# A new hand-written order and more choices of engine in a block-sparse attention and channel-mix kernel

## The chip, the cores and the metric

The kernel runs on one core of one Trainium2 chip. The metric is the device time of one execution in microseconds (us). Its engines are TensorE (PE in the rows; PEld is its weight load), VectorE (DVE), ScalarE (ACT), GpSimd (POOL) and SyncE (SP), which issues every DMA here.

## The reference

Two layers follow each other. The first is block-sparse attention: 4 batches, 8 heads, 768 positions in 24 blocks of 32, head size 64. A query block sees its neighbours, the first and last block, and three blocks drawn at random; the first and the last query block see everything.

```python
scores = scale * np.matmul(q, k.transpose(0, 1, 3, 2))
mask = np.abs(blk_i - blk_j) <= window
mask = mask | (blk_i == 0) | (blk_j == 0) | (blk_i == n_blocks - 1) | (blk_j == n_blocks - 1)
...
attn = attn / (np.sum(attn, axis=-1, keepdims=True) + 1e-09)
return np.matmul(attn, v).astype(np.float32)
```

The second mixes channels of its output x (4 x 768 x 512) with the position before:

```python
xk = mu_k * x + (1.0 - mu_k) * x_prev
xr = mu_r * x + (1.0 - mu_r) * x_prev
k = np.maximum(xk @ w_k, 0.0)
v = k * k @ w_v
r = 1.0 / (1.0 + np.exp(-(xr @ w_r)))
return (r * v).astype(np.float32)
```

w_k is 512 x 1024, w_v 1024 x 512, w_r 512 x 512; all three come as 8-byte floats.

## The kernel before, in words

**Attention** goes in 26 units. Units 0 to 21 each take one query block of all four batches (near units); units 22 to 25 take the first and last block of one batch (wide units). A near unit is a chain: load queries, keys and values; two score steps on PE (tile s, L400, 64 recorded matmuls in all: an fp32 matmul of the program is recorded as two); a row maximum on DVE (tile nm, L410); four exponentials on ACT (tile p); a transpose on DVE (tile r, L453); a DMA that moves it (tile pt); two value steps on PE (tile o, L473, 128 recorded matmuls; L434 in units 0 to 2); the division on DVE, and a turn of x into the mixer's tile xt ("put x").

**The mixer** takes 12 tiles of 256 positions. For each, xk and xr are mixed (ACT "now", DVE "mix", L663) and split into a high and a low part ("hi" on ACT, "lo" on POOL, L672). PE then computes r (gate, tile r_0p or r_1p, 12 matmuls of 512 columns a half tile, L696), h (hidden, four tiles h_0p to h_3p of 24 matmuls of 256 columns, L713) and v (values, 24 matmuls of 512 columns a half tile, in 8 steps of 3, L742). Between h and v stand relu and "hi" on ACT, "square" (L728) and "lo" (L730) on POOL. PE's result tiles of the mixer take turns in two buffers of one tag, "m".

**Weights**: 20 pieces w0 to w19 are converted from 8-byte floats on DVE, ACT and POOL (size, tail, sign, join, hi, lo) early in the program.

**The order.** Each step is recorded by plan.add with its engine, an estimated time and its buffers. The list ORDER then names the steps one by one, and they are issued in just that order, engine by engine; CHOICE names the engine of a step that is recorded by choose with several ways. Nothing is planned at run time: a step waits on its engine until its inputs and buffers are there, and all steps behind it on that engine wait too.

**PE's instruction stream.** A recorded matmul is two instructions, a weight load and a matmul. With the waits on semaphores that stand between them the built program before has 14,654 instructions on PE, one straight stream without loops.

Of the kernel before, what the change touches and what calls it, by code (L numbers as in the profile page):

```python
# [15 lines left out]
ALU = mybir.AluOpType  # L16
# [4 lines left out]
B, H, S, D = 4, 8, 768, 64  # L21
# [74 lines left out]
def block_sparse_attention_channel_mix(  # L96
# [3 lines left out]
    nc = tc.nc  # L100
# [13 lines left out]
    def choose(name, ways, **more):  # L114

        way = CHOICE.get(name, 0)
        engine, ns, port, fn = ways[way]
        plan.add(name, engine, ns, fn, port=port, ways=[w[:3] for w in ways], **more)
# [45 lines left out]
    def warm(times, ns):  # L164
        w = buf([P, 512], F32, "m", M_BUFS, f"warm{times}", ps)

        def run():
            one = nc.const_aps.tensor(1.0, (P, 512), BF16)
            for i in range(times):
                nc.tensor.matmul(w.ap, one[:, 0:P], one, start=(i == 0), stop=(i == times - 1))  # L170

        plan.add("warm", PE, ns * times, run, writes=[(w,)], code=2 * times)
# [4 lines left out]
    def weight(i, name, src):  # L177
# [37 lines left out]
        choose(f"w{i} tail", [(DVE, 338, 338, tail), (POOL, 650, 0, tail_pool), (ACT, 600, 0, tail_act)], reads=[(raw,)], writes=[(f, 0)])  # L215
# [13 lines left out]
        choose(f"w{i} sign", [(DVE, 338, 338, sign), (ACT, 600, 0, sign_act), (POOL, 650, 0, sign_pool)], reads=[(raw,)], writes=[(f, 1)])  # L229
# [151 lines left out]
    def near_unit(at, q, first, o):  # L381
# [6 lines left out]
        for gi in range(2):  # L388
# [30 lines left out]
            for i in range(4):  # L419
                row, a = divmod(i, 2)  # L420
                plan.add(f"u{name} exp {i}", ACT, 420, lambda p=p, s=s, nm=nm, row=row, a=a, i=i: nc.scalar.activation(
                    p.ap[:, i * 256 : (i + 1) * 256].rearrange("p (c x j) -> p c x j", c=2, j=QB),
                    s.ap[:, row, a * 256 : (a + 1) * 256].rearrange("p (c j x) -> p c x j", c=2, j=QB), AF.Exp, bias=nm.ap[:, i : i + 1], scale=SCALE),
                    reads=[(s,), (nm,)], writes=[(p, i)], table="exp")
# [120 lines left out]
    def finish(at, members, o, parts):  # L545
# [3 lines left out]
        for i in range(len(o)):  # L549
# [7 lines left out]
            plan.add(f"u{at} {i} recip", DVE, 275, recip, reads=[(o[i], *parts)], writes=[(R, i)])  # L557
# [12 lines left out]
            plan.add(f"u{at} {i} divide", DVE, 430, divide, reads=[(o[i], *parts), (R, i)], writes=[(x, i)])  # L570
        n = members[0][1]
        if moved:
# [4 lines left out]
            def move():  # L577
                for b in range(B):
# [4 lines left out]
            plan.add(f"u{at} put x", ACT, 467, lambda: nc.scalar.copy(to.ap[:, :, n % 2, :, 1:], xm.ap.rearrange("p b c x -> p c b x")),  # L583
                     reads=[(xm,)], writes=[(to, n)])
# [11 lines left out]
        if not n:  # L596
# [12 lines left out]
        plan.add(f"u{at} put x", ACT, 467, lambda: nc.scalar.copy(  # L609
            to.ap[:, :, n % 2, :, 1:], tp.ap.rearrange("p c (b x) -> p c b x", b=B)), reads=[(tp,)], writes=[(to, n)])  # L610
# [27 lines left out]
    def split_x(t, which, i0, many, name):  # L638
# [14 lines left out]
        for h in range(CC // MIX):  # L653
            f = buf([P, MIX, tw], F32, "mix", 1, f"{name}f{h}")
            for i in range(MIX):
# [6 lines left out]
                def mix(d=d, c=c, i=i, f=f):  # L662
# [7 lines left out]
            plan.add(f"{name} hi {h}", ACT, 66 + 0.895 * MIX * tw, lambda f=f, cs=cs: nc.scalar.copy(dst.ap[:, 0, cs], f.ap),  # L670
                     reads=[(f, *range(MIX))], writes=[(dst, (0, h))])
            plan.add(f"{name} lo {h}", POOL, 160 + 2.17 * MIX * tw, lambda f=f, cs=cs: nc.gpsimd.tensor_tensor(  # L672
                out=dst.ap[:, 1, cs], in0=f.ap, in1=dst.ap[:, 0, cs], op=ALU.subtract),
                reads=[(f, *range(MIX)), (dst, (0, h))], writes=[(dst, (1, h))])
# [15 lines left out]
    def gate(name, xr, z, last):  # L690
# [12 lines left out]
        plan.add(f"{name} out", ACT, 475, lambda: nc.scalar.copy(z.ap, pr.ap[:, 0:512]), reads=[(pr,)], writes=[(z,)])  # L703

    def hidden(name, xk, k2, f2, last):
# [17 lines left out]
        def lo():  # L723
# [4 lines left out]
        plan.add(f"{name} square", POOL, 1000, lambda: nc.gpsimd.tensor_tensor(out=kk.ap, in0=kk.ap, in1=kk.ap, op=ALU.mult),  # L728
                 reads=[(kk,)], writes=[(kk,)])
        plan.add(f"{name} lo", POOL, 1245, lambda: nc.gpsimd.tensor_tensor(out=lo(), in0=kk.ap, in1=hi(), op=ALU.subtract),  # L730
                 reads=[(kk,), (k2, (0, f2))], writes=[(k2, (1, f2))])
# [74 lines left out]
MIX = 2  # L806
# [9 lines left out]
}  # L816
ORDER = [
# [128 lines left out]
```

## Time and profile before

| | |
|---|---|
| Runs (us) | 538.75, 540.99, 534.01; median 538.75 |
| Profiled execution | 541.3 us, span 539.4 us |
| Mean granted TensorE clock | 0.978 |
| PE / DVE / ACT / POOL busy (us) | 486.6 / 291.5 / 327.0 / 215.4 |
| Matmuls recorded | 7260 |
| DMA | 115.68 MB, 214 GB/s |

The span runs from the first to the last instruction; the execution's own time is 1.9 us longer. Busy time of PE is modelled from pipelined matmuls, so the time of a stretch of matmuls is best read from the start of its first row to the start of the next row.

### The profile page before, as it was taken

The page shows a single profiled execution, that of the slowest core. Times are in us where ns is not written, and L with a number is a line of the kernel's source. Part 1 is how long each engine was busy: PE and PEld are TensorE (multiplying, and loading weights), DVE is VectorE, ACT ScalarE, POOL GpSimd, SP SyncE. Part 2 cuts the span into 40 slices and gives each one's busy share as a digit, 9 for nine tenths or more (in the row PEclk, how much of TensorE's full clock was granted, in tenths as well). Part 3 has the DMA queues.
Part 4 walks back from the last instruction along what each step waited for, and adds up shares of the span by engine and source line. Part 5 has one row for each costly group of instructions (what it writes and reads, how often), then busy time and mean ns, then how long its engine had stood idle before and what let it go on. Part 6 is the DMA issues. An engine that isn't in the chain of part 4 may idle for free.

```text
span 539.4 us, 17745 instructions
## 1 busy us (share of the span) xinstructions
PE 486.6 (90%) x7260; PEld 398.7 (74%) x7260; DVE 291.5 (54%) x560; ACT 327.0 (61%) x749; POOL 215.4 (40%) x208
## 2 busy tenths in 40 slices
PE   0585999899999999998999996998999999999997
PEld 0253578668887778786887885877878878888896
DVE  3795879655655653666355565466454363222221
ACT  4685878756664665676484575492644866455541
POOL 4464556212521712442620641351441632726361
PEclk9996999998999999999999999899999999999999
DMA  8999699897878888787798888489966655101001
GB/s 286 403 377 396 203 343 296 272 259 213 235 220 221 259 222 236 237 245 232 219 254 235 243 217 281 116 258 279 307 187 182 222 118 133 46 2 39 21 21 39
DMA packets 58627, 115.68 MB, mean 214 GB/s; under 512 B 7729, under 2 KB 20785, under 8 KB 55602
## 3 DMA queue, kind: packets, MB, share of 16 engines
q1 hardware_dynamic: 58546, 114.55, 69.8%
q8 instruction: 57, 0.93, 0.7%
q14 instruction: 24, 0.20, 0.1%
HBM read 77.82 MB, written 6.29 MB: 156 GB/s over the span
## 4 chain that ended last, share of the span: by engine, by line
PE 68%; DMA 9%; SPq 7%; issue 5%; DVE 5%; ACT 4%; POOL 0%; DVEq 0%; ACTq 0%; POOLq 0%
PE v L742 19%; PE s L400 7%; PE h_1p L713 6%; PE h_0p L713 6%; PE o L473 5%; PE r_1p L696 5%; PE h_3p L713 5%; PE r_0p L696 5%; PE h_2p L713 4%; DMA pt<-r 3%; SPq L461 3%; PE o L536 2%; PE sw L494 2%; DMA KA<-kt 2%; DVE r L453 2%
## 5 line engine op out<-in xcount | busy, mean ns | idle before, releaser
L742 PE MATMUL v<-w,k 128*128 128x512 f32 (+1 forms) x600 | 140.3, 386 | 0.0
L742 PEld LDWEIGHTS v<-w,k 128*128 128x128 f32 x600 | 107.6, 188 | 25.0 <-issue 1.8
L400 PE MATMUL s<-KA,q 64*32 64x256 f32 x1408 | 54.2, 424 | 27.3 <-DMA KA<-kt 18.2
L450 ACT ACTIVATE p<-s,nm 128x256 f32<-128x256 f32 x152 | 65.0, 478 | 1.6 <-DVE R L554 0.8
L400 PEld LDWEIGHTS s<-KA,q 64*32 64x32 f32 x1408 | 28.1, 116 | 45.0 <-issue 18.5
L410 DVE TENSOR_REDUCE nm<-s 128x4 f32<-128x1024 f32 x44 | 53.1, 1214 | 14.8 <-PE s L400 14.6
L453 DVE STREAM_TRANSPOSE r<-p 128x1024 f32<-128x1024 f32 x38 | 46.1, 1229 | 12.4 <-DMA pt<-r 6.7
L473 PE MATMUL o<-VA,pt 128*32 128x65 f32 x2432 | 41.5, 221 | 10.8 <-issue 8.2
L672 POOL TENSOR_TENSOR xr<-xr_0f,xr 128x256 fp32r<-128x256 f32 x24 | 17.8, 742 | 83.2 <-ACT xr L670 76.4
L473 PEld LDWEIGHTS o<-VA,pt 128*32 128x32 f32 x2432 | 36.7, 109 | 19.1 <-issue 14.4
L663 DVE SCALAR_TENSOR_TENSOR xr_1f<-xt,mk,xr_1d 128x128 f32<-128x128 f32 x48 | 21.9, 457 | 41.9 <-ACT xr_1d L660 24.7
L672 POOL TENSOR_TENSOR xr<-xr_1f,xr 128x256 fp32r<-128x256 f32 x24 | 17.8, 743 | 55.3 <-ACT xr L670 55.3
L713 PE MATMUL h_0p<-xk,w 128*128 128x256 f32 x288 | 38.9, 290 | 0.5 <-DVE w L244 0.3
L713 PEld LDWEIGHTS h_0p<-xk,w 128*128 128x128 f32 x288 | 36.7, 195 | 3.2 <-issue 1.2
L565 DVE TENSOR_TENSOR x<-o,R 128x128 f32<-128x128 f32 x96 | 25.0, 323 | 25.2 <-ACT xt L583 11.9
L713 PE MATMUL h_1p<-xk,w 128*128 128x256 f32 x288 | 37.9, 287 | 0.0
L713 PE MATMUL h_3p<-xk,w 128*128 128x256 f32 x288 | 37.6, 284 | 0.0
L713 PE MATMUL h_2p<-xk,w 128*128 128x256 f32 x288 | 37.5, 284 | 0.0
L713 PEld LDWEIGHTS h_1p<-xk,w 128*128 128x128 f32 x288 | 36.1, 194 | 1.6 <-DVE xr_1f L663 0.8
L663 DVE SCALAR_TENSOR_TENSOR xr_0f<-xt,mk,xr_0d 128x128 f32<-128x128 f32 x48 | 17.8, 371 | 35.5 <-ACT xr_0d L660 16.1
L713 PEld LDWEIGHTS h_3p<-xk,w 128*128 128x128 f32 x288 | 35.7, 190 | 1.4 <-issue 0.8
L696 PE MATMUL r_0p<-w,xr 128*128 128x512 f32 x144 | 36.2, 398 | 0.5 <-POOL xr L672 0.5
(174 smaller groups left out, 842.4 us busy)
## 6 DMA issues: line engine op xcount, KB each, us to landing
VA<-vt SPq DMA_DIRECT2D x92, 260.0 KB, 4.3
KA<-kt SPq DMA_DIRECT2D x89, 256.0 KB, 4.1
pt<-r SPq DMA_DIRECT2D x76, 256.0 KB, 4.9
VA<-vw SPq DMA_DIRECT2D x24, 260.0 KB, 5.1
KA<-kq SPq DMA_DIRECT2D x16, 384.0 KB, 5.9
ptw<-rw SPq DMA_DIRECT2D x32, 192.0 KB, 3.9
out<-z SPq DMA_DIRECT2D x23, 256.0 KB, 4.2
q<-qt SPq DMA_DIRECT2D x22, 256.0 KB, 4.6
```

The source lines that it names most:

```text
L400: nc.tensor.matmul(s.ap[ROWS[j], row, a * 256 : (a + 1) * 256].rearrange("p (n x) -> p n x", x=BLK), q.ap[half, (hp * QB + j) * BLK : (hp ...
L410: nc.vector.tensor_reduce(out=nm.ap.rearrange("p (r a) -> p r a", r=2), in_=s.ap.rearrange("p r (a x) -> p r a x", a=2), axis=AX.X, op=ALU ...
L450: plan.add(f"u{name} exp {i}", ACT, 365, lambda row=row, a=a, i=i: nc.scalar.activation(squares()[:, :, :, i, :], s.ap[:, row, a * 256 : ( ...
L453: plan.add(f"u{name} turn", DVE, N_TURN, lambda: nc.vector.transpose(out=r.ap[:, :, gi].rearrange("p j c i x -> p j (c i x)"), in_=squares ...
L461: nc.sync.dma_start(pt.ap[:, b].rearrange("p g c i x -> p (g c i x)"), r.ap[ROWS[b]].rearrange("p j g c i x -> p j (g c i x)"))
L473: nc.tensor.matmul(o[gi].ap[ROWS[j], i * DV : (i + 1) * DV], pt.ap[:, j, gi, g, 2 * row + a, :], VA.ap[:, c0 + g, j, h * DV : (h + 1) * DV ...
L565: nc.vector.tensor_tensor(out=to[:, :, 2 * e : 2 * e + 2], in0=o[i].ap.rearrange("p (c e v) -> p c e v", e=2, v=DV)[:, :, e, 0:D].rearrang ...
L663: nc.vector.scalar_tensor_tensor(out=parts(f.ap[:, i, :]), in0=cols(c, 1), scalar=mk.ap[:, 2 + which, c : c + 1], in1=parts(d.ap), op0=ALU ...
L672: plan.add(f"{name} lo {h}", POOL, 160 + 2.17 * MIX * tw, lambda f=f, cs=cs: nc.gpsimd.tensor_tensor(out=dst.ap[:, 1, cs], in0=f.ap, in1=d ...
L696: nc.tensor.matmul(pr.ap[:, 0:512], xr.ap[:, a, c, :], weight_of["r", c].ap[:, w, :], start=(c == 0 and m == 0), stop=(c == CC - 1 and m = ...
L713: nc.tensor.matmul(ph.ap[:, ff * TT : (ff + 1) * TT], weight_of["k", c, f2 // 2].ap[:, w, f % 4 * P : (f % 4 + 1) * P], xk.ap[:, a, c, :], ...
L742: nc.tensor.matmul(pv.ap[:, 0:width], k2.ap[:, a, f, i * P : (i + 1) * P], weight_of["v", f].ap[:, w, cs], start=(f == 0 and m == 0), stop ...
```

## The change

The 2,106 steps and what they compute stay the same. ORDER is a new list, CHOICE another table, and steps of 13 kinds stand on another engine. Against before, in the built program: 32 "lo" and 21 "square" of h go from POOL to DVE; 24 "lo" of xr and 15 of xk from POOL to DVE; 22 "hi" of xr and 12 of xk from ACT to POOL; 14 copies of r out of PSUM ("r out") and 8 "put x" from ACT to DVE; some 46 conversion steps of the weights and 5 "turned" copies between ACT, DVE and POOL. The warm-up matmuls are 10 instead of 20 and stand in another place. Estimates of time (ns) that the list was made with are changed too; they have no effect on the program.

```diff
-        def run():
+        def run(times):
...
-        plan.add("warm", PE, ns * times, run, writes=[(w,)], code=2 * times)
+        choose("warm", [(PE, ns * many, 0, lambda many=many: run(many)) for many in (times, times // 2, 1)], writes=[(w,)], code=2 * (times, times // 2, 1)[CHOICE.get("warm", 0)])
...
+            choose(f"{name} hi {h}", [
+                (ACT, 66 + 0.895 * MIX * tw, 0, lambda f=f, cs=cs: nc.scalar.copy(dst.ap[:, 0, cs], f.ap)),
+                (POOL, 50 + 1.05 * MIX * tw, 0, lambda f=f, cs=cs: nc.gpsimd.tensor_copy(dst.ap[:, 0, cs], f.ap)),
+            ], reads=[(f, *range(MIX))], writes=[(dst, (0, h))])
+            choose(f"{name} lo {h}", [
+                (POOL, 160 + 2.17 * MIX * tw, 0, lambda rest=rest: rest(nc.gpsimd)),
+                (DVE, 63 + 1.06 * MIX * tw, 63 + 1.06 * MIX * tw, lambda rest=rest: rest(nc.vector)),
+            ], reads=[(f, *range(MIX)), (dst, (0, h))], writes=[(dst, (1, h))])
...
+        choose(f"{name} out", [
+            (ACT, 475, 0, lambda: nc.scalar.copy(z.ap, pr.ap[:, 0:512])),
+            (DVE, 600, 0, lambda: nc.vector.tensor_copy(out=z.ap, in_=pr.ap[:, 0:512])),
+        ], reads=[(pr,)], writes=[(z,)])
...
+        choose(f"{name} square", [
+            (POOL, 1000, 0, lambda: nc.gpsimd.tensor_tensor(out=kk.ap, in0=kk.ap, in1=kk.ap, op=ALU.mult)),
+            (DVE, 603, 603, lambda: nc.vector.tensor_tensor(out=kk.ap, in0=kk.ap, in1=kk.ap, op=ALU.mult)),
+        ], reads=[(kk,)], writes=[(kk,)])
+        choose(f"{name} lo", [
+            (POOL, 1245, 0, lambda: nc.gpsimd.tensor_tensor(out=lo(), in0=kk.ap, in1=hi(), op=ALU.subtract)),
+            (DVE, 603, 603, lambda: nc.vector.tensor_tensor(out=lo(), in0=kk.ap, in1=hi(), op=ALU.subtract)),
+        ], reads=[(kk,), (k2, (0, f2))], writes=[(k2, (1, f2))])
...
 ORDER = [
-    3, 4, 1, 961, 7, 16, 933, 934, 935, 936, 937, 938, 11, 14, 939, 982, 975, 964, 13, 978, 962, 984, 963, 977, 985, 10, 976, 979, 8, 5, 12, 20, 9, 965, 966, 980, 15, 919, 55,
+    3, 4, 11, 0, 13, 1, 7, 919, 16, 9, 975, 921, 1045, 12, 978, 976, 1046, 961, 14, 10, 1048, 5, 1047, 977, 1049, 979, 980, 981, 962, 1050, 964, 963, 965, 1051, 920, 982, 922,
```

First place: PE around the scores of unit 7. o5_0 and o5_1 are the values of unit 5, s7_0 and s7_1 the scores of unit 7, v1 the values of mixer tile 1; a row of x16 or x32 is recorded as twice as many matmuls. Before:

```order
L742 MATMUL v1_0_0_1488<-w18_1561,k21_1219 128x512 x3
L473 MATMUL o5_0_1613<-VA_68,pt5_1496 32x65 x32
L473 MATMUL o5_1_1651<-VA_68,pt5_1496 32x65 x32
L400 MATMUL s7_0_1688<-KA_67,q7_1231 32x256 x16
L400 MATMUL s7_1_1705<-KA_67,q7_1231 32x256 x16
L742 MATMUL v1_1_0_1726<-w12_661,k21_1219 128x512 x3
```

Of the change:

```order
L759 MATMUL v1_1_0_1517<-w17_749,k21_1292 128x512 x3
L472 MATMUL o5_0_1606<-VA_68,pt5_1558 32x65 x32
L472 MATMUL o5_1_1639<-VA_68,pt5_1558 32x65 x32
L759 MATMUL v1_0_0_1568<-w15_873,k21_1292 128x512 x3
L759 MATMUL v1_1_0_1517<-w18_1555,k21_1292 128x512 x3
L759 MATMUL v1_1_0_1517<-w19_127,k21_1292 128x512 x3
L399 MATMUL s7_0_1712<-KA_67,q7_1454 32x256 x16
L399 MATMUL s7_1_1731<-KA_67,q7_1454 32x256 x16
```

Nine matmuls of 512 columns now stand between the values and the scores, which stood back to back.

Second place: PE around the values of unit 19 (o19) and the scores of unit 21 (s21). Before:

```order
L696 MATMUL r7_0p_5262<-w3_97,xr7_0_5200 128x512 x3
L473 MATMUL o19_0_5278<-VA_68,pt19_5229 32x65 x32
L473 MATMUL o19_1_5330<-VA_68,pt19_5229 32x65 x32
L400 MATMUL s21_0_5365<-KA_67,q21_4904 32x256 x16
L400 MATMUL s21_1_5382<-KA_67,q21_4904 32x256 x16
```

Of the change:

```order
L706 MATMUL r7_0p_5253<-w3_361,xr7_0_5026 128x512 x3
L726 MATMUL h7_0p_5238<-xk7_4898,w4_1036 128x256 x3
L726 MATMUL h7_0p_5238<-xk7_4898,w5_1166 128x256 x3
L726 MATMUL h7_0p_5238<-xk7_4898,w6_1148 128x256 x3
L726 MATMUL h7_0p_5238<-xk7_4898,w7_171 128x256 x3
L472 MATMUL o19_0_5296<-VA_68,pt19_5276 32x65 x32
L472 MATMUL o19_1_5334<-VA_68,pt19_5276 32x65 x32
L399 MATMUL s21_0_5401<-KA_67,q21_5329 32x256 x16
L399 MATMUL s21_1_5424<-KA_67,q21_5329 32x256 x16
```

Here values and scores still follow each other; twelve matmuls of h now stand between r7_0 and the values, and 14 more recorded matmuls stand ahead of o19_1 in the program.

Third place: DVE around the row maxima of unit 10 (nm10). Before:

```order
L453 STREAM_TRANSPOSE r9_2371<-p9_1_2232 128x4x256
L410 TENSOR_REDUCE nm10_0_2395<-s10_0_2354 128x4
L663 SCALAR_TENSOR_TENSOR xr3_0f0_2491<-xt3_1724,mk_70,xr3_0d1_2350 128x128
L748 SCALAR_TENSOR_TENSOR z2_0_1844<-v2_0_0_2284,z2_0_1844 128x512
L453 STREAM_TRANSPOSE r9_2371<-p9_0_2133 128x4x256
```

Of the change:

```order
L675 TENSOR_TENSOR xr3_0_2228<-xr3_0f0_2361,xr3_0_2228 128x256
L452 STREAM_TRANSPOSE r9_2445<-p9_1_2333 128x4x256
L765 SCALAR_TENSOR_TENSOR z2_1_2230<-v2_1_0_2298,z2_1_2230 128x512
L409 TENSOR_REDUCE nm10_0_2520<-s10_0_2486 128x4
L666 SCALAR_TENSOR_TENSOR xr3_1f0_2522<-xt3_1563,mk_70,xr3_1d0_2467 128x128
L409 TENSOR_REDUCE nm10_1_2539<-s10_1_2503 128x4
L715 COPY z3_0_2568<-r3_0p_2525 128x512
```

The row L675 is a "lo" that was POOL's, the row L715 an "r out" that was ACT's; both now stand in DVE's queue among the attention's steps.

## Rows read from the trace of the kernel before

**Rows 1.** The page: span, and busy us of each engine.

```profile
span 539.4 us, 17745 instructions
...
PE 486.6 (90%) x7260; PEld 398.7 (74%) x7260; DVE 291.5 (54%) x560; ACT 327.0 (61%) x749; POOL 215.4 (40%) x208
```

**Rows 2.** Windows: stretch and length, busy us by engine, granted clock, DMA share, GB/s.

```profile
16.75:60.00 43.25, 30.54 (x699) 19.45 (x699) 33.46 (x62) 31.21 (x76) 21.51 (x23) 0.84 0.95 358
60.00:100.00 40.00, 38.25 (x616) 29.37 (x617) 34.04 (x59) 30.73 (x73) 24.09 (x22) 1.00 0.93 295
100.00:340.00 240.00, 223.30 (x3793) 183.72 (x3791) 135.71 (x267) 149.25 (x354) 79.16 (x75) 0.98 0.83 238
340.00:536.20 196.20, 194.54 (x2156) 166.10 (x2156) 81.39 (x158) 107.99 (x237) 83.37 (x78) 0.99 0.45 131
```

**Rows 3.** Waits of PE on "issue": us in total, times, longest.

```profile
PE o L473 <- issue: 8.2, 5, 4.4
PE s L400 <- issue: 7.7, 6, 1.7
PE o L434 <- issue: 4.2, 1, 4.2
```

**Rows 4.** The page's DMA queues: packets, MB, share of 16 engines.

```profile
q8 instruction: 57, 0.93, 0.7%
```

**Rows 5.** Timeline of PE, 90 to 140: start, us, operation; idle before in brackets.

```profile
90.67 3.02 PE L696 MATMUL r_1p<-w,xr 128*128 128x512 f32 x12
93.53 0.85 PE L742 MATMUL v<-w,k 128*128 128x512 f32 x3
...
101.01 2.04 PE L473 MATMUL o<-VA,pt 128*32 128x65 f32 x128
102.97 1.49 PE L400 MATMUL s<-KA,q 64*32 64x256 f32 x39
105.93 1.07 PE L400 MATMUL s<-KA,q 64*32 64x256 f32 x25 [1.46 <-issue]
106.93 6.52 PE L742 MATMUL v<-w,k 128*128 128x512 f32 x27
...
130.06 3.00 PE L713 MATMUL h_1p<-xk,w 128*128 128x256 f32 x24
132.99 1.96 PE L400 MATMUL s<-KA,q 64*32 64x256 f32 x64
134.88 1.80 PE L473 MATMUL o<-VA,pt 128*32 128x65 f32 x110
137.09 0.53 PE L473 MATMUL o<-VA,pt 128*32 128x65 f32 x18 [0.41 <-issue]
137.55 3.11 PE L713 MATMUL h_3p<-xk,w 128*128 128x256 f32 x24
```

**Rows 6.** The chain in order of time, 116 to 127: start, us, what.

```profile
122.40 4.44 PE h_0p L713 x24
```

**Rows 7.** Timeline of PE, 336 to 344.

```profile
336.06 0.32 PE L473 MATMUL o<-VA,pt 128*32 128x65 f32 x1 [4.42 <-issue]
336.31 3.67 PE L400 MATMUL s<-KA,q 64*32 64x256 f32 x64
339.90 3.97 PE L713 MATMUL h_1p<-xk,w 128*128 128x256 f32 x24
```

**Rows 8.** Timeline of PE, 65 to 71: the warm-up matmuls.

```profile
65.36 4.55 PE L170 MATMUL warm<-const-bfloat16-1.0 128*128 128x512 bf16 x20
...
70.71 0.30 PE L473 MATMUL o<-VA,pt 128*32 128x65 f32 x2 [0.37 <-DMA pt<-r]
```

**Rows 9.** Groups of DVE instructions: busy us, mean ns, idle before by releaser.

```profile
L410 DVE TENSOR_REDUCE nm<-s 128x4 f32<-128x1024 f32 x44 | 53.1, 1214 | 14.8 <-PE s L400 14.6 <-ACT pt L373 0.2
L453 DVE STREAM_TRANSPOSE r<-p 128x1024 f32<-128x1024 f32 x38 | 46.1, 1229 | 12.4 <-DMA pt<-r 6.7 <-ACT p L450 3.9 <-DMA q<-qt 1.6
L748 DVE SCALAR_TENSOR_TENSOR z<-v,z 128x512 f32<-128x512 f32 x23 | 15.8, 687 | 19.1 <-PE v L742 14.0 <-ACT z L775 4.1 <-ACT p L450 0.7
```

More of the change, by code (lines that the diff above doesn't have):

```diff
@@ L114, in choose @@
     def choose(name, ways, **more):
-        way = CHOICE.get(name, 0)
-        engine, ns, port, fn = ways[way]
+        engine, ns, port, fn = ways[CHOICE.get(name, 0)]
         plan.add(name, engine, ns, fn, port=port, ways=[w[:3] for w in ways], **more)
@@ L213, in tail_act @@
                 nc.scalar.activation(halves(U16, 0), shorts(1), AF.Copy, scale=2.0**-13, bias=2.0**-14 - 0.5)
-        choose(f"w{i} tail", [(DVE, 338, 338, tail), (POOL, 650, 0, tail_pool), (ACT, 600, 0, tail_act)], reads=[(raw,)], writes=[(f, 0)])
+        choose(f"w{i} tail", [(DVE, 338, 338, tail), (POOL, 900, 0, tail_pool), (ACT, 640, 0, tail_act)], reads=[(raw,)], writes=[(f, 0)])
         def sign():
@@ L227, in sign_pool @@
                 nc.gpsimd.tensor_scalar(out=halves(F16, 1), in0=high().bitcast(F32), scalar1=2.0**-60, scalar2=None, op0=ALU.mult)
-        choose(f"w{i} sign", [(DVE, 338, 338, sign), (ACT, 600, 0, sign_act), (POOL, 650, 0, sign_pool)], reads=[(raw,)], writes=[(f, 1)])
+        choose(f"w{i} sign", [(DVE, 338, 338, sign), (ACT, 630, 0, sign_act), (POOL, 1650, 0, sign_pool)], reads=[(raw,)], writes=[(f, 1)])
         def join():
@@ L420, in near_unit @@
                 row, a = divmod(i, 2)
-                plan.add(f"u{name} exp {i}", ACT, 420, lambda p=p, s=s, nm=nm, row=row, a=a, i=i: nc.scalar.activation(
+                plan.add(f"u{name} exp {i}", ACT, 365, lambda p=p, s=s, nm=nm, row=row, a=a, i=i: nc.scalar.activation(
                     p.ap[:, i * 256 : (i + 1) * 256].rearrange("p (c x j) -> p c x j", c=2, j=QB),
@@ L555, in recip @@
                 nc.vector.reciprocal(r, r)
-            plan.add(f"u{at} {i} recip", DVE, 275, recip, reads=[(o[i], *parts)], writes=[(R, i)])
+            plan.add(f"u{at} {i} recip", DVE, 330, recip, reads=[(o[i], *parts)], writes=[(R, i)])
             def divide(i=i, each=each):
@@ L568, in divide @@
                         in1=R.ap[:, each, :].rearrange("p (c e) (z o) -> p c e z o", e=2, z=1)[:, :, e].to_broadcast([P, 2, 2, BLK]), op=ALU.mult)
-            plan.add(f"u{at} {i} divide", DVE, 430, divide, reads=[(o[i], *parts), (R, i)], writes=[(x, i)])
+            plan.add(f"u{at} {i} divide", DVE, 460, divide, reads=[(o[i], *parts), (R, i)], writes=[(x, i)])
         n = members[0][1]
@@ L582, in finish @@
             to, then = tile_of(n // 2), tile_of((n + 1) // 2)
-            plan.add(f"u{at} put x", ACT, 467, lambda: nc.scalar.copy(to.ap[:, :, n % 2, :, 1:], xm.ap.rearrange("p b c x -> p c b x")),
-                     reads=[(xm,)], writes=[(to, n)])
+            choose(f"u{at} put x", [
+                (ACT, 467, 0, lambda: nc.scalar.copy(to.ap[:, :, n % 2, :, 1:], xm.ap.rearrange("p b c x -> p c b x"))),
+                (DVE, 600, 600, lambda: nc.vector.tensor_copy(out=to.ap[:, :, n % 2, :, 1:], in_=xm.ap.rearrange("p b c x -> p c b x"))),
+            ], reads=[(xm,)], writes=[(to, n)])
             plan.add(f"u{at} put z", ACT, 80, lambda: nc.scalar.copy(
@@ L608, in finish @@
         to = tile_of(n // 2)
-        plan.add(f"u{at} put x", ACT, 467, lambda: nc.scalar.copy(
-            to.ap[:, :, n % 2, :, 1:], tp.ap.rearrange("p c (b x) -> p c b x", b=B)), reads=[(tp,)], writes=[(to, n)])
+        choose(f"u{at} put x", [
+            (ACT, 467, 0, lambda: nc.scalar.copy(to.ap[:, :, n % 2, :, 1:], tp.ap.rearrange("p c (b x) -> p c b x", b=B))),
+            (DVE, 600, 0, lambda: nc.vector.tensor_copy(out=to.ap[:, :, n % 2, :, 1:], in_=tp.ap.rearrange("p c (b x) -> p c b x", b=B))),
+        ], reads=[(tp,)], writes=[(to, n)])
         then = tile_of((n + 1) // 2)
@@ L669, in split_x, with rest @@
             cs = slice(h * MIX, (h + 1) * MIX)
[L670 to L674, printed above, removed]
+            def rest(by, f=f, cs=cs):
+                by.tensor_tensor(out=dst.ap[:, 1, cs], in0=f.ap, in1=dst.ap[:, 0, cs], op=ALU.subtract)
+            choose(f"{name} hi {h}", [
[6 more added lines that the diff above has]
+            ], reads=[(f, *range(MIX)), (dst, (0, h))], writes=[(dst, (1, h))])
         return dst
@@ L702, in gate @@
                      reads=[(xr, *SPLIT), *[(weight_of["r", c], 0, 1) for c in cs]], writes=[(pr,)], code=12)
-        plan.add(f"{name} out", ACT, 475, lambda: nc.scalar.copy(z.ap, pr.ap[:, 0:512]), reads=[(pr,)], writes=[(z,)])
+        choose(f"{name} out", [
+            (ACT, 475, 0, lambda: nc.scalar.copy(z.ap, pr.ap[:, 0:512])),
+            (DVE, 600, 0, lambda: nc.vector.tensor_copy(out=z.ap, in_=pr.ap[:, 0:512])),
+        ], reads=[(pr,)], writes=[(z,)])
     def hidden(name, xk, k2, f2, last):
@@ L727, in hidden @@
         plan.add(f"{name} hi", ACT, 522, lambda: nc.scalar.activation(hi(), kk.ap, AF.Square), reads=[(kk,)], writes=[(k2, (0, f2))])
[L728 to L731, printed above, removed]
+        choose(f"{name} square", [
[6 more added lines that the diff above has]
+        ], reads=[(kk,), (k2, (0, f2))], writes=[(k2, (1, f2))])
     def values(t, i, k2, z, last):
```

159 rows, old and new, of tables (CHOICE, ORDER) are left out of this document.

## The prediction

> **What bounds the kernel now.** I read the windows first, because the limits differ by stage. TensorE (PE) is busy 486.6 of 539.4 us [rows 1], so 52.8 us of idle time are what an order can win. Of them 16.7 lie before the first scores, 12.7 from there to 60 us (43.25 less 30.54, at a DMA share of 0.95 and a clock of 0.84), 1.8 up to 100, 16.7 between 100 and 340, 1.7 after that, and 3.2 behind the last matmul [rows 2]. The early part belongs to the transfers, the late part is full. So I looked at the 16.7 us between 100 and 340, where DVE is busy 136 of 240 us and the DMA share is 0.83: nothing else is full there.
>
> The waits give the cause: PE waited 15.9 us on "issue" (8.2 and 7.7, eleven times) in scores and values of moved units, and 4.2 us once in L434 [rows 3]. "Issue" is time in which an engine waits for nothing that the profile shows. In the timeline such a pause cuts a run of equal matmuls in two, 39 scores and 25 scores of one unit [rows 5]: their inputs were there, or the first would not have run. What was missing is the instructions. The instruction queue carried 57 packets in 0.93 MB [rows 4], 16 KB each; the program has 14,654 instructions on PE, 257 to a packet. I counted the instructions of the program up to each pause: all twelve stand at number 449 to 451 beyond a multiple of 512, so at every second packet. I call these places borders; there are 28.
>
> Not every border pauses. Ahead of those that do, the 256 instructions (128 matmuls) before the border are all scores and values, which run fast: values 1.96 us for 128 (101.01 to 102.97), scores 1.89 for 64 (132.99 to 134.88) [rows 5]. With 89 values and 39 scores the 128 take 2.5 us. Where 12 matmuls of r (some 2.8 us, 0.23 each) lie among them, as at 94 us, PE goes on at once [rows 5]. So I take it that a packet is asked for about when those 256 begin, and comes late if they last less than it needs. Adding the time of the 256 to the pause behind them gives what each of the eleven needed: 2.8 to 4.9 us for ten, 6.6 for the one at 336.06 [rows 7].
>
> The Trainium skill says otherwise ("Runtime: NRT & Kernel Launch", section Instruction fetch mechanics): fetch streams ahead in blocks of 256 instructions and is hidden, and PE holds 2048 of them. The block size agrees with [rows 4]; the hidden fetch does not, by the eleven pauses of [rows 3]. By that rule the spacing of this order would be worth nothing; it is a rival below.
>
> **The change part by part.**
>
> Borders. With the same 512 and the same offset I counted where the borders fall in the new order, and added up the 128 matmuls before each at the rates above (v and r 0.23 us, h 0.12). At the fifteen borders from unit 7 to unit 19, which had 2.0 to 2.9 us, now 4.3 to 7.6 us lie ahead: nine v matmuls between values and scores at unit 7, twelve of h before the values of unit 19. If the packet needs what it needed, ten of eleven would have 0.4 us or less to wait, and the long one 1 to 2. Spread over fifteen borders that is about 3 us left.
>
> What is taken away is more than the 15.9 us of idle time, since a row's end is modelled: from 102.97 to 106.93 a unit's scores take 3.96 us against 1.89, a pause of 2.07 where the bracket says 1.46; from 134.88 to 137.55 the values take 2.67 against 1.96, 0.71 where it says 0.41 [rows 5]. Half of 0.61 and 0.30 is 0.45, for eleven pauses 5 us. **So 20.9 us go, and 3 stay.**
>
> The clock. After the long pause PE is slow: 64 scores take 3.67 us against 1.96, 24 matmuls of h 3.97 against 3.00 [rows 5, 7], and after the pause at 120 us 24 of h take 4.44 [rows 6]. Together 1.7 + 1.0 + 1.4, **4 us, go with the pauses.** In the stretch the granted clock is 0.98 [rows 2].
>
> Head borders. The pause in L434 (4.2 us) stands where 105 values and 19 scores now come before the border: 2.7 us, as before. I leave it. One border on, at unit 4's scores, 12 matmuls of r lay ahead; these have gone behind the scores, and 2.6 us are left, against 4.1 in the middle of the needs. **Plus 1.6 us**, bounds 0 and 4.2.
>
> Warm-up. Ten matmuls of 4.55/20 us less stand in the stream; the ten that stay are early, where PE waits anyway. What they covered is the wait for unit 3's move, still 0.37 us at 70.71 [rows 8]. That move is 0.5 MB earlier in SP's queue, 1.5 us at 358 GB/s [rows 2]. So **minus 1.5 us** of the 2.3; bounds 0 and 2.3.
>
> The transfers of the head. Up to unit 0's drawn keys 4.82 MB are queued instead of 4.56, 0.7 us later; up to unit 2's drawn values 17.1 instead of 18.2, 3 us earlier; unit 0's and 1's values stay. **Nothing**, bounds 3 us either way. That PE's early steps are covered by transfers hides the new order of weight conversions too; without that cover their bound would be the 12.7 us of idle time.
>
> Steps on another engine. A 128 x 512 step on DVE takes 0.69 us [rows 9]. The 53 steps of h and 15 of xk are 47 us, 24 of xr at half the size 8, 14 "r out" and 8 "put x" 15: DVE goes from 291 to about 361 us, 70% of the span. Of that some 35 fall into 100 to 340, 171 of 220 us there. POOL and ACT get lighter. On PE's path this costs nothing so long as DVE has slack; that cover is 49 us in that stretch.
>
> New waits. A stretch that is 20 us shorter asks the same transfers in less time: 0.83 x 240/220 is a share of 0.91. Between 60 and 100 the share is 0.93 and PE idles 1.8 of 40 us [rows 2], which over 220 us would be 10; at the share of now it is the 0.8 us that are not "issue". I take **plus 4 us**, bounds 0 and 10, nearer the low end because DVE, which is at 85% between 60 and 100, is less full here.
>
> Sum: 539.4 - 20.9 - 4 + 3 + 1.6 - 1.5 + 4 = 521.6 us of span, 523.5 with the 1.9 us around it. The profiled execution, 541.3 us, is 2.55 above the median of 538.75, so I forecast **521 us**. The bounds around it: residual pauses 0 to 9 (half of the old ones), new waits 0 to 10, head 4 either way, hence 512 to 531.
>
> **The rivals.**
>
> *More is won.* If no new waits and no residual pauses come and the head border falls away too, the 3, the 4, the 1.6 and 4.2 us more go: about 508 to 512. For it: PE idles only 1.8 us from 60 to 100, where more borders lie and a slow product stands before each [rows 2]. Against: a packet needed over 6 us twice, here and in the head. 15%.
>
> *Half is won.* The packets share the DMA engines with data; at a share of 0.91 they come later, and the transfers behind PE's steps bind in place of the fetches (new waits of 10 us, pauses of 7). Then 521 + 6 + 4, about 531. For it speaks the idle time at 0.93; against, PE's 38 of 40 us there. 17%.
>
> *It does not do what it says.* The pauses would be something else than fetches and come at other places, as many as before: 538.75 - 1.5, about 537. Against it are twelve of twelve pauses at one remainder. 3%. The section of the Trainium skill that is named above leads to this case.
>
> *Slower.* DVE becomes what PE waits for. PE's mixer results take turns in two buffers; fourteen of them, the "r out", now wait in DVE's queue behind a row maximum (1.21 us) and a transpose (1.23 us) [rows 9], where ACT emptied them. Once DVE runs a whole product (2.8 us) late, each of the fourteen holds PE for up to 2.4 us, 34 in all: 521 + 34 = 555. It decides from the point at which DVE is over some 95% busy in a stretch; the fullest now is 85% [rows 2], and the middle would be 78%. 6%.
>
> **How the numbers follow.** The forecast has 59%. For the range, 511 to 533 holds nearly all of the forecast's own 512 to 531, half of the first rival and most of the second; about 0.17 is left out. Faster by over 2% means below 528, which is about what a measurement here can tell: 0.53 of the forecast, 0.15, and 0.06 of the half win give 0.74. Within 2%: 0.06, 0.11 and 0.03, so 0.20. Slower 0.06.
>
> **What would show it.** PE's waits on "issue" from 100 on fall from 15.9 us to under 5; PE is busy over 95% between 100 and 320, at a granted clock of 0.99 or more; the last unit's scores start 20 us sooner. DVE's busy time rises to some 360 us, and no wait of PE for DVE is over 2 us in total. If the pauses stay where the count puts the borders, though 4 us and more lie ahead, the reading of how long a packet needs is wrong; if they come elsewhere, the reading of borders is. If PE waits for DMA by over 10 us after 60 us, the half win is right.

## The result, and the profile after

| | before | changed |
|---|---|---|
| Runs (us), median | 539.87 (4 runs) | 522.42 (519.11 to 523.59, 4 runs) |
| Ratio | | 0.9702, 95% interval 0.9605 to 0.9799 |
| Profiled execution, span | 541.3, 539.4 | 523.59, 521.8 |
| Mean granted clock | 0.978 | 0.984 |

The change makes the kernel faster by 3.0%; 521 us was forecast. The profiled execution of the kernel before is one of its slower ones (its runs took 534.0 to 546.1 us). The page of the changed kernel, span and busy us of each engine, answers to [rows 1]:

```profile
span 521.8 us, 17723 instructions
...
PE 481.7 (92%) x7250; PEld 396.1 (76%) x7250; DVE 349.0 (67%) x675; ACT 304.4 (58%) x695; POOL 129.8 (25%) x147
```

Its windows answer to [rows 2]. The middle stretch is drawn 20 us shorter; some 110 recorded matmuls more lie behind its end than before, which cost the last stretch 1.2 us of busy time:

```profile
16.00:60.00 44.00, 31.26 (x716) 19.63 (x722) 35.75 (x69) 31.63 (x76) 20.02 (x22) 0.91 0.96 354
60.00:100.00 40.00, 35.68 (x589) 28.89 (x589) 33.31 (x60) 30.56 (x71) 16.11 (x15) 0.93 0.96 306
100.00:320.00 220.00, 218.52 (x3681) 181.73 (x3685) 160.99 (x315) 136.32 (x325) 45.23 (x49) 1.00 0.86 248
320.00:518.00 198.00, 195.77 (x2283) 165.53 (x2273) 110.95 (x217) 99.17 (x215) 42.59 (x49) 0.99 0.49 142
```

From 100 to 320 us PE idles 1.5 us, where it idled 16.7 between 100 and 340. The gain is there. From 60 to 100 it idles 4.3 us instead of 1.8, and the clock is 0.93 instead of 1.00: some of it is given back. Ahead of 60 us it is the other way round, 0.91 where it was 0.84. PE's waits on "issue", against [rows 3] (the 2.1 us are 0.64 at 38, 1.09 at 92 and 0.38 at 137 us):

```profile
PE o L433 <- issue: 3.8, 1, 3.8
PE s L399 <- issue: 2.1, 3, 1.1
```

The timeline of PE at unit 7, where [rows 5] had 1.46 us of idle inside the scores, and at unit 19, where [rows 7] had 4.42 us inside the values:

```profile
103.65 2.03 PE L472 MATMUL o<-VA,pt 128*32 128x65 f32 x128
105.61 2.38 PE L759 MATMUL v<-w,k 128*128 128x512 f32 x9
107.92 1.96 PE L399 MATMUL s<-KA,q 64*32 64x256 f32 x64
109.81 1.67 PE L759 MATMUL v<-w,k 128*128 128x512 f32 x6
...
317.74 1.55 PE L726 MATMUL h_0p<-xk,w 128*128 128x256 f32 x12
319.23 2.03 PE L472 MATMUL o<-VA,pt 128*32 128x65 f32 x128
321.76 1.96 PE L399 MATMUL s<-KA,q 64*32 64x256 f32 x64 [0.51 <-DMA KA<-kt]
323.65 3.12 PE L726 MATMUL h_3p<-xk,w 128*128 128x256 f32 x24
```

The 64 scores take 1.96 us at both places (3.67 after the long pause before), and 24 of h 3.12 instead of 3.97: the clock stays up. What is lost stands at 60, 93 and 98 us:

```profile
59.93 3.80 PE L399 MATMUL s<-KA,q 64*32 64x256 f32 x64 [1.05 <-ACT xt L611]
63.66 4.04 PE L706 MATMUL r_0p<-w,xr 128*128 128x512 f32 x12
...
91.46 0.64 PE L399 MATMUL s<-KA,q 64*32 64x256 f32 x9
93.19 1.93 PE L399 MATMUL s<-KA,q 64*32 64x256 f32 x55 [1.09 <-issue]
...
99.96 0.51 PE L759 MATMUL v<-w,k 128*128 128x512 f32 x1 [1.47 <-ACT xt L615]
```

Three waits of 0.5 to 1.1 us come close together at 56 to 60 us, and from 59.1 to 65.9 us the granted clock is 0.50, the lower of its two levels: scores and r run at about half speed, some 2.8 us more than at full clock. Unit 6's scores have a pause that they did not have, and at 98 us the values wait 1.5 us for "put z" on ACT (L615), the step that hands the last position of each block of x to the next tile.

### The profile page after: what moved, and what is told of

Its sections match the earlier page's. It is cut to its first block, busy times and chain, and to the rows that moved or that the text cites. A ratio compares the mean times of both kernels' runs of the same rounds, so it can differ in the third digit from the quotient of the medians.

```text
span 521.8 us, 17723 instructions
## 1 busy us (share of the span) xinstructions
PE 481.7 (92%) x7250; PEld 396.1 (76%) x7250; DVE 349.0 (67%) x675; ACT 304.4 (58%) x695; POOL 129.8 (25%) x147
## 4 chain that ended last, share of the span: by engine, by line
PE 66%; SPq 11%; DMA 9%; ACT 6%; DVE 4%; issue 4%; POOL 0%; DVEq 0%; ACTq 0%; POOLq 0%
PE v L759 18%; PE s L399 6%; PE h_3p L726 6%; PE r_1p L706 5%; PE h_2p L726 5%; PE h_1p L726 5%; PE r_0p L706 5%; PE h_0p L726 5%; SPq L460 5%; PE o L472 4%; DMA KA<-kt 4%; PE o L535 2%; PE sw L493 2%; SPq L578 2%; DMA xm<-rx 1%
## 5 line engine op out<-in xcount | busy, mean ns | idle before, releaser
L399 PE MATMUL s<-KA,q 64*32 64x256 f32 x1408 | 49.8, 408 | 21.4 <-DMA KA<-kt 17.9
L449 ACT ACTIVATE p<-s,nm 128x256 f32<-128x256 f32 x152 | 63.5, 478 | 0.6
L472 PE MATMUL o<-VA,pt 128*32 128x65 f32 x2432 | 39.9, 221 | 1.5 <-DMA pt<-r 1.4
L666 DVE SCALAR_TENSOR_TENSOR xr_1f<-xt,mk,xr_1d 128x128 f32<-128x128 f32 x48 | 17.8, 371 | 30.4 <-ACT xr_1d L663 28.1
L726 PE MATMUL h_0p<-xk,w 128*128 128x256 f32 x288 | 37.8, 286 | 0.0
L726 PEld LDWEIGHTS h_2p<-xk,w 128*128 128x128 f32 x288 | 35.4, 190 | 1.6 <-ACT h_0k L739 0.6
L706 PE MATMUL r_1p<-w,xr 128*128 128x512 f32 x144 | 36.5, 399 | 0.0
L726 PE MATMUL h_1p<-xk,w 128*128 128x256 f32 x288 | 36.4, 282 | 0.0
L706 PEld LDWEIGHTS r_0p<-w,xr 128*128 128x128 f32 x144 | 27.2, 194 | 7.2 <-issue 1.2
```

Of the source, the lines that this page charges most:

```text
L399: nc.tensor.matmul(s.ap[ROWS[j], row, a * 256 : (a + 1) * 256].rearrange("p (n x) -> p n x", x=BLK), q.ap[half, (hp * QB + j) * BLK : (hp ...
L449: plan.add(f"u{name} exp {i}", ACT, 365, lambda row=row, a=a, i=i: nc.scalar.activation(squares()[:, :, :, i, :], s.ap[:, row, a * 256 : ( ...
L472: nc.tensor.matmul(o[gi].ap[ROWS[j], i * DV : (i + 1) * DV], pt.ap[:, j, gi, g, 2 * row + a, :], VA.ap[:, c0 + g, j, h * DV : (h + 1) * DV ...
L666: nc.vector.scalar_tensor_tensor(out=parts(f.ap[:, i, :]), in0=cols(c, 1), scalar=mk.ap[:, 2 + which, c : c + 1], in1=parts(d.ap), op0=ALU ...
L706: nc.tensor.matmul(pr.ap[:, 0:512], xr.ap[:, a, c, :], weight_of["r", c].ap[:, w, :], start=(c == 0 and m == 0), stop=(c == CC - 1 and m = ...
L726: nc.tensor.matmul(ph.ap[:, ff * TT : (ff + 1) * TT], weight_of["k", c, f2 // 2].ap[:, w, f % 4 * P : (f % 4 + 1) * P], xk.ap[:, a, c, :], ...
```

## The experiments

Theory A says that the gain is that of the instruction fetches; theory B, that it comes from the steps on other engines and from the order as such. All ratios are to the kernel before, timed beside each run. Its median was 539.8 us beside before_pad110, before_pad256, after_pad216 and order_before_choice_after, 535.0 beside before_split, before_pad56, order_after_choice_before and after_pad64, and 540.9 beside the last three, so microseconds of different groups can differ by 1% by themselves; those of the changed kernel are from the result above.

| Run | us | Ratio, 95% interval |
|---|---|---|
| before_pad110 | 542.07 | 1.0050 (1.0000 to 1.0099) |
| before_pad256 | 540.54 | 1.0013 (0.9964 to 1.0062) |
| after_pad216 | 523.84 | 0.9756 (0.9694 to 0.9818) |
| order_before_choice_after | 544.69 | 1.0129 (1.0054 to 1.0204) |
| before_split | 548.78 | 1.0232 (1.0145 to 1.0319) |
| before_pad56 | 524.47 | 0.9794 (0.9719 to 0.9870) |
| order_after_choice_before | 544.89 | 1.0176 (1.0097 to 1.0254) |
| after_pad64 | 528.19 | 0.9847 (0.9770 to 0.9923) |
| after_two_pads | 520.69 | 0.9645 (0.9591 to 0.9699) |
| order_before_choice_after_pad56 | 534.25 | 0.9898 (0.9837 to 0.9960) |
| after_weights_before | 527.88 | 0.9778 (0.9718 to 0.9839) |

**Shifting the borders alone.** Five runs put N tiny matmuls ahead of everything, into PE's wait for the first keys. 256 of them keep PE busy for 7.1 us of the first 16.75.

```diff
+    one = nc.const_aps.tensor(1.0, (P, 512), BF16)
+    for part in range(2):
+        w = buf([P, 512], F32, "m", M_BUFS, f"pad{part}", ps)
+        for i in range(N // 2):
+            nc.tensor.matmul(w.ap[0:BLK, 0:8], one[:, 0:BLK], one[:, 0:8], start=(i == 0), stop=(i == N // 2 - 1))
     for op in plan.order():
         op.fn()
```

> The kernel before with 110 tiny matmuls (32 columns of weights, 8 columns moving) ahead of all others, while PE waits for the first keys; they shift every border by 220 instructions. By the count no border past the head then has less than 4.2 us of matmuls ahead. Theory A (the gain is that of the borders): PE's waits on issue after 100 us fall from 15.9 us to under 3, and the time from about 540 to 514 to 522 us, though order and engines are those of before. Theory B (the gain comes from the steps on other engines and from the order in general, the pauses only change their place): 537 to 541 us.

It was not faster. Theory A as I had put it failed, and the timeline says how. At unit 14's scores:

```profile
214.53 2.03 PE L473 MATMUL o<-VA,pt 128*32 128x65 f32 x128
216.49 1.49 PE L400 MATMUL s<-KA,q 64*32 64x256 f32 x38
219.91 1.08 PE L400 MATMUL s<-KA,q 64*32 64x256 f32 x26 [1.92 <-issue]
```

The pauses are still there. Counted in the program all but one of them stand at 194 to 196 beyond a multiple of 512, where before they stood at 450 or 451 (the one at 384 us still does). These are the packets that I had passed over: 450 less 194 is 256. So every packet of 256 instructions ends at a border, not every second. In the old order a unit and the mixer steps beside it fill about 512 instructions, so one border in two fell upon fast matmuls, the same one each time. A shift by 220 instructions brought the other there. Call this theory A': PE pauses at a border of 256 if the 128 matmuls ahead of it are all fast.

> A control: the same with 256 tiny matmuls, 512 instructions, so that every border past the head stands where it stood among the steps. Theory A: the eleven pauses past 100 us are back at the same steps, 15 us of waits on issue or more, and the time is within 1.5% of before (533 to 546 us). If the tiny matmuls as such help (a warmer clock, another head), it is faster by more than that.

Same time, and the pauses are back at 450 or 451: the tiny matmuls as such do nothing.

> The kernel before with 56 tiny matmuls at the start: borders shift by 112 instructions, less than half the 256 between two packets. By the count six borders past 60 us keep 2.0 to 3.9 us ahead and the others 4 and more. Theory A': 8 to 15 us faster than before, 525 to 532 us, with 2 to 7 us of waits on issue past 100 us. If borders were at every 512 instructions, seven or more pauses would stay, 534 to 541 us.

It came out just under the low end in microseconds; against the 535.0 us timed beside it the gain is 10.5 us, within the 8 to 15. This shift is not near a multiple of 128 matmuls, and it gives 2.1 of the 3.0% with order and engines untouched. Two pauses are left past 60 us:

```profile
PE s L400 <- DMA KA<-kt: 17.4, 4, 14.7
PE o L473 <- DMA pt<-r: 3.5, 5, 1.4
...
PE h_1p L713 <- issue: 2.2, 1, 2.2
...
PE o L473 <- issue: 0.7, 1, 0.7
```

> The changed kernel with 216 tiny matmuls at the start: the borders shift by 432 instructions, back among values and scores; seven borders past 60 us then have 2.0 to 3.6 us ahead. Theory A: 8 to 12 us slower than the changed kernel, 530 to 535 us, with 6 to 10 us of waits on issue after 60 us. Theory B: as the changed kernel, 519 to 524 us.

> The changed kernel with 64 tiny matmuls at the start, 128 instructions, which by the count is its worst phase: nine borders past 60 us have 2.1 to 2.8 us ahead. Theory A': 6 to 12 us slower than the changed kernel, 528 to 534 us. The run with 216 tiny matmuls was only 1.4 us slower with seven such borders counted; if this one is slower by less than 3 us as well, what lies ahead in matmuls is not the whole condition.

The first missed: 1.4 us over the changed kernel, not 8 to 12. It has four pauses past 100 us with 4.0 us of idle, but in the head L433 waits 1.9 us on issue instead of 3.8. The second is 5.8 us over the changed kernel, at the low end; it has seven pauses at borders with 10.6 us of idle in all, five of them past 100 us. By the ratios the two are 0.5 and 1.5% slower than the changed kernel; the intervals overlap, so in time neither is shown, and the pauses are what the traces show. The changed kernel can be made to pause again, but less than the old one: its scores and values stand mostly in runs of 64 or 128, only five of them in 192.

**How much must lie ahead.** From the 13 traces I counted the borders between 100 and 340 us by the time that the 128 matmuls ahead took:

| Time of the 128 ahead | Borders | Paused 0.3 us or more | Longest |
|---|---|---|---|
| under 3 us | 75 | 58 | 4.6 us |
| 3 to 4 us | 7 | 2 | 2.9 us |
| 4 to 9 us | 154 | 4 | 1.2 us |

Here the time ahead runs from the start of the first of the 128 to the start of the last, and a pause from that start to the next; borders with more ahead are left out. A short time ahead makes a pause likely, not certain.

**The packets themselves.** That the missing thing is instructions was so far argued from the count. The traces settle it: they hold every packet of the queue q8 [rows 4], 16 KB each, one for each border behind the first. In the kernel before:

| Packet starts (us) | Has landed | PE goes on behind the pause |
|---|---|---|
| 43.18 | 44.15 | 45.52 |
| 103.41 | 104.48 | 105.93 |
| 119.31 | 120.19 | 121.78 |
| 333.71 | 334.66 | 336.06 |

In the 13 traces 80 of the 83 pauses on "issue" of 0.25 us or more stand at a border and end 1.0 to 1.6 us after its packet has landed, and none of the 734 borders that could be followed is passed sooner than 0.96 us after that. The other three stand at the first matmuls of a unit's values (2.8 us in after_pad64, 1.7 in after_weights_before, 2.1 in order_before_choice_after_pad56); no fetch is shown behind them, and their cause is open. The packets also tell the 17 that did not pause from the 58: in the 17 the packet had started between 2.5 us ahead of the border before and 0.2 us behind it; in 57 of the 58 it started 0.1 to 4.2 us behind it. What sets that moment was not tried.

**Order and engines apart.** One run has the old ORDER with the new CHOICE, one the new ORDER with the old CHOICE.

```diff
 # order_before_choice_after: the changed kernel with
-    "warm": 1, "u0 0 1 turned": 1, "u0 1 0 turned": 1, ...
+    "u0 0 1 turned": 1, "u0 1 0 turned": 1, ...
-    3, 4, 11, 0, 13, 1, 7, 919, 16, 9, ...
+    3, 4, 1, 961, 7, 16, 933, 934, 935, 936, ...
```

> The old order with the new engines of all steps (the warm-up stays at 20); the borders lie as before, fifteen of them with 2.0 to 3.1 us ahead. Theory A: no gain, 533 to 546 us. Theory B: most of the gain of 17 us, 520 to 528 us.

> The new order with the old engines of all steps (warm-up as in the new one): the runs of fast matmuls are split as in the changed kernel. Theory A': most of the gain stays, 520 to 528 us, less what the old engines cost PE in waits for POOL and ACT. If the gain needs the steps on other engines: 533 to 545 us.

Neither part alone gains: both are slower than before by 1.3 to 1.8%, yet together they are 3.0% faster. With the old order the pauses stay (waits on issue of 9.3 and 5.7 us). With the new order and the old engines the pauses past 50 us are gone, as A' says, but the time did not follow; this run spoke against the expectation. Its windows:

```profile
0.00:100.00 100.00, 64.17 (x1282) 47.20 (x1284) 68.82 (x130) 66.27 (x150) 49.65 (x53) 0.91 0.90 311
100.00:320.00 220.00, 213.05 (x3584) 175.11 (x3583) 133.13 (x254) 144.49 (x343) 80.01 (x76) 1.00 0.84 241
320.00:537.00 217.00, 207.31 (x2398) 174.26 (x2383) 92.23 (x176) 115.46 (x256) 85.43 (x81) 0.99 0.49 144
```

PE idles 7.0 us in the middle (1.5 in the changed kernel) and 9.7 in the last stretch (2.2), and the waits have other names:

```profile
PE v L759 <- ACT z L714: 3.3, 3, 1.9
...
PE r_0p L706 <- ACT xr L678: 1.4, 1, 1.4
```

L714 is the "r out" on ACT. The new order has 14 of them on DVE.

> The changed kernel with the old engines for the 46 conversion steps of the weights alone; attention and mixer keep the new ones. The new order with all old engines took 544.9 us. If the steps of attention and mixer on DVE are what the new order needs: 522 to 527 us. If it is the weights, whose conversion is ahead of the mixer's start: 533 to 545 us, with the loss before 100 us.

With the old engines for the weights alone 5.5 of the 22.5 us are lost (0.8 of 4.7% by the ratios). That is just above the first case's range, and the loss lies where the second put it, ahead of 100 us, where PE is busy 63.1 us instead of 66.9. The remaining 17 us hang on the steps of attention and mixer; which of them was not tried.

> The old order with the new engines, which took 544.7 us, and 56 tiny matmuls at the start as in the run that brought the old kernel from 540 to 524.5 us. If the pauses add to whatever else the engines do: 12 to 17 us faster than without the tiny matmuls, 528 to 533 us. If the new engines in the old order put other waits in place of the pauses: 537 us or more.

The shift takes 10.4 us off, a little less than expected in microseconds (2.3% by the ratios). Past 60 us two pauses remain at borders, 1.25 us at 72 and 2.58 at 331 us; an idle time of 2.05 us on "issue" at 275 us is none of them, its packet had landed 9.7 us earlier. The pauses cost time with either set of engines.

**Spacing alone.** In the old ORDER, at fifteen units the slow products ahead were put between the two fast pairs, with the steps that depend on them:

```diff
 # PE's steps at units 5 and 7, by name
-v1_0_0 4, v1_0_0 5, v1_0_0 6, u5 0 values, u5 1 values, u7 0 scores, u7 1 scores
+u5 0 values, u5 1 values, v1_0_0 4, v1_0_0 5, v1_0_0 6, u7 0 scores, u7 1 scores
```

> The kernel before, engines and start as they were; in its order alone, at the fifteen near units whose values and scores stand back to back (192 fast matmuls), the 2.1 to 2.9 us of slow matmuls that stood ahead of the four steps are put between the two pairs, with the steps that depend on them. Theory A' (every 256 instructions is a border; PE pauses where the 128 matmuls ahead of it are all fast, whatever the phase): waits on issue past 100 us fall from 15.9 us to under 4, and the time by 14 to 21 us, to 519 to 526 us. Theory B' (spacing alone is not enough, the rest of the new order and the engines carry the gain): 530 to 541 us.

The pauses are gone past 60 us, and it is 2.3% slower: B' had the direction, and the size is outside both. PE reaches the values sooner than their transfers:

```profile
98.09 0.30 PE L473 MATMUL o<-VA,pt 128*32 128x65 f32 x2
99.81 0.30 PE L473 MATMUL o<-VA,pt 128*32 128x65 f32 x2 [1.42 <-DMA pt<-r]
...
116.21 3.63 PE L473 MATMUL o<-VA,pt 128*32 128x65 f32 x122 [1.39 <-DMA pt<-r]
```

The waits for pt, in the kernel before and in this run (total, times, longest):

```profile
PE o L473 <- DMA pt<-r: 2.5, 4, 1.5
PE o L473 <- DMA pt<-r: 9.8, 12, 1.6
```

Twelve waits of 9.8 us in all stand in place of the pauses. The slow products had been the cover of the move; behind the values they cover nothing. Two waits for keys (tile KA) of 2.07 us at 181 and 4.07 us at 247 us come on top. In three places of the middle the granted clock then falls to its lower level, from 116.3, 249.4 and 304.0 us on; the 122 values in 3.63 us are one of them, the same 122 take 2.01 us at 101 and 166 us.

**Pauses of the head moved.** The changed kernel with 88 tiny matmuls at the start and 40 ahead of unit 2's turn of x, together 256 instructions:

```diff
+    tiny(88, "a")
     for op in plan.order():
+        if op.name == "u2 turn x":
+            tiny(40, "b")
         op.fn()
```

> The changed kernel with 88 tiny matmuls at the start and 40 more ahead of unit 2's turn of x, where PE waits some 2 us for DVE in the changed kernel. Together they are 256 instructions, so past 60 us the borders stand where they stood, and no border there has under 4 us of matmuls ahead; in the head the three borders that paused (2.2, 1.0 and 4.0 us) get another place. If those pauses are on the path: 2 to 5 us faster than the changed kernel, 517 to 521 us. If the head is set by its transfers whatever PE does: 521 to 524 us.

The pauses of the head are gone, one of 0.47 us at 90 us is left. The profiled execution took 519.23 us. At 0.9645 (0.9591 to 0.9699) it is the fastest run here, but its interval overlaps that of the changed kernel: faster than before is shown, faster than the changed kernel is not.

## Why the prediction was right

**Pauses.** 20.9 us were to go and 3 to stay. The mechanism was the one forecast: the packets above show the fetch, and one starts about when the 256 instructions ahead begin. Past 100 us one pause of 0.38 us idle is left, about 1 us with the slower scores behind it. The term was right and 2 us too careful. The step "at every second packet" was wrong, as before_pad110 showed. Past 60 us it cost the sum nothing: at the borders that I had left out, the changed kernel takes 7 us and more for the 128 matmuls ahead. That is luck, since they were not counted; in the head the pause of 0.64 us at 38 us stands at one of them.

**The clock.** 4 us were to come back in the middle stretch: the granted clock there is 1.00, and the matmuls behind both places run at full rate. Not foreseen was that scores and r would lose 2.8 us to the lower level at 60 us; ahead of that the clock is higher than before (0.91 for 0.84), so not all of it is a loss against the kernel before.

**The head.** L433 pauses 3.8 us against 4.2, left as it was. Unit 4's scores did not pause (1.6 us too many), unit 6's did. The wait behind the warm-up matmuls is still there, as it was to be with ten of them gone:

```profile
68.70 0.30 PE L472 MATMUL o<-VA,pt 128*32 128x65 f32 x2 [0.38 <-DMA pt<-r]
69.47 0.72 PE L472 MATMUL o<-VA,pt 128*32 128x65 f32 x36 [0.46 <-DMA pt<-r]
```

**New waits.** Plus 4 us was the term. PE idles 2.5 us more between 60 and 100, 0.5 more in the last stretch, and some 0.3 more in the middle beside the pause left there, 3.3 in all; 1.1 of them are unit 6's pause, which is no new wait. So the term was nearly twice too large, and its place was wrong: not the transfers of the middle, but ACT's "put z" ahead of 100 us. The errors, each 2 to 3 us, cancel; that a span of 521.8 meets 521.6 is luck, the steps are not as close. One sign of the forecast failed: the scores of the last near unit were to start 20 us sooner if that was the unit meant, and start 14.6 sooner (321.76 against 336.31); those of the last wide unit start 13 sooner.

**Steps on another engine.** DVE was to rise to 361 us and rose to 349.0. A square or an "r out" of 128 x 512 took about 0.68 us, as taken from [rows 9]; the 32 "lo" of h took more, 0.68 to 0.84. The total is lower because "mix" took less than before (0.37 instead of 0.46 us each on one of its two tiles) and for reasons that were not traced:

```profile
L743 DVE TENSOR_TENSOR h_0k<-h_0k 128x512 f32<-128x512 f32 x7 | 4.8, 680 | 3.1 <-ACT k L740 3.0
L715 DVE COPY z<-r_0p 128x512 f32<-128x512 f32 x7 | 4.8, 679 | 2.7 <-PE r_0p L706 2.6
```

DVE is 73% busy in the middle, and PE waits for it 1.9 us in all, so the slower rival did not come. But "costs nothing" said too little. I had treated the engines as neutral to the gain; with the old engines the same order is 22.5 us slower. The forecast held because the change brings both.

**The rivals.** "Does not do what it says" is out: shifting the stream by 56 tiny matmuls moves the time by 2% and the pauses with it, and the pauses end a fixed time after a packet. "Half is won" did not come either: from 100 to 320 us the DMA share is 0.86, not 0.91, and PE idles 1.5 us. The section of the Trainium skill that the prediction names ("Runtime: NRT & Kernel Launch", Instruction fetch mechanics) has blocks of 256 instructions, which the borders bear out, and a hidden fetch, which 58 pauses in 75 do not.

## What to carry to other kernels

Idle time on "issue" inside a run of equal matmuls is worth counting in instructions: if such places share a remainder and each resumes a fixed time after an instruction packet has landed, it is the fetch. Some instructions put into idle time at the start can move it, though only a test at a second shift shows the period. A pause that goes is a gain only where the next input is already there, so the order around it and the engines that feed it have to be changed together. Work that is put between fast steps must not be the work that covered a transfer.

## What the runs showed of the hardware

PE's instructions came in packets of 256 (16 KB, 0.9 to 1.9 us on the queue in the kernel before). No border between two packets was passed sooner than 0.96 us after the next packet had landed, and that packet started between 2.8 us ahead of the border before and 4.7 us behind it (borders from 100 to 340 us of all traces); a pause there lasted up to 4.6 us past 100 us. A tiny matmul with its weight load, 32 columns of weights and 8 moving, took 28 ns on average (256 in 7.11 us).
